# First chunk of an mLSTM cell with a feed-forward block: another order of weight parts, values and quarters, and sums of three with fewer copies

## The chip, the cores and the metric

The kernel runs on one core of a Trainium2 chip. The metric is device time in microseconds (us) of that core, the median of several executions. A profile of one execution gives the start, length and releaser of each instruction on each engine: TensorE (PE; its weight loads are PEld), VectorE (DVE), ScalarE (ACT), GpSimd (POOL) and SyncE (SP), which issues the transfers.

## The reference, cut to what matters

An mLSTM cell runs over 768 steps for 4 batches of 8 heads with 40 values each; its output, seen as 3072 rows of 320, goes through two matrices of weights with a quick GELU between them. All inputs are float32.

```python
for t in range(S):                                  # S = 768; B = 4, H = 8, D = 40
    kt, vt, qt = (k[:, :, t], v[:, :, t], q[:, :, t])
    m_new = np.maximum(f_gate[:, :, t] + m, i_gate[:, :, t])
    f_stab = np.exp(f_gate[:, :, t] + m - m_new)
    i_stab = np.exp(i_gate[:, :, t] - m_new)
    m = m_new
    C = f_stab[:, :, None, None] * C + i_stab[:, :, None, None] * np.einsum('bhd,bhe->bhde', vt, kt)
    n = f_stab[:, :, None] * n + i_stab[:, :, None] * kt
    h_tilde = np.einsum('bhde,bhe->bhd', C, qt)
    nq = np.einsum('bhd,bhd->bh', n, qt)[:, :, None]
    y[:, :, t] = h_tilde / np.maximum(np.abs(nq), 1.0) / (1.0 + np.exp(-o_gate[:, :, t]))
x = y.transpose(0, 2, 1, 3).reshape(B * S, H * D)   # 3072 x 320
h = x @ w_in                                        # w_in 320 x 2048
out = (h / (1.0 + np.exp(-1.702 * h))) @ w_out      # w_out 2048 x 320
```

## The kernel before, in words

The 768 steps are cut into 6 chunks (`w`) of 128. Within a chunk the recurrence is written as attention: for each batch `b`, `weights(w, b)` gives the decay of each pair of steps, `scores(w, b)` the products of keys and queries on TensorE, which VectorE multiplies into the decay (L353), and `values(w, b)` the products of that with v (L363), followed on VectorE by the denominator and the output gate (L390 to L396) and on POOL by a copy of the last 64 columns of the row `y` (L398). `seam(w, b)` transposes `y` on TensorE (L405) and ScalarE copies it into the columns of batch `b` in `xT` (L406). The feed-forward block follows: `up` and then `down`. From chunk 1 on, both products are run by a scheme with seven products instead of eight, and the attention of the next chunk is run between the blocks of `down`.

The order of the instructions on each engine is the order in which the program names them; every engine has its own queue and works it off in that order, and waits are put where one instruction needs another's data or buffer. All that the change touches lies in the first chunk, whose calls stand one after another at L665 to L736.

The first chunk has its own ways. Keys and queries of batch `b` are transposed on TensorE into PSUM and copied by ScalarE (`transposes(0, b)`, L308 and L311). The decay is formed on TensorE from two rows of numbers, minus the gate sum `a3` and the running maximum `m3`, each held as a sum of three bfloat16 on 3 times 32 partitions, and ScalarE takes the exponential (L325 to L331). `gates(0)` makes these sums of three: POOL those of `a3` (L252 to L256), VectorE those of `m3` (L262 to L267). Each part is made in `part`, copied to its 32 partitions, and subtracted from what is left.

The matrices of weights come as float32 and are converted on the chip, in 20 pieces of 128 x 512. `convert(n, "A")` is ScalarE's part of a piece (L228, the high half, and L229, the low half), `convert(n, "V")` is VectorE's (L232 to L237), which needs both; `convert(n)` names both parts. SP issues the loads of all pieces in one queue together with those of k, q, v and the gates, and pieces 10 and later are loaded into the room of earlier ones once these are converted.

For the first two column blocks of `up` the kernel doesn't wait for all four batches: `full_rows(j, c, t)` multiplies the rows of two batches (half `t`) for one block `j` and one of two parts `c` of the inner dimension, two matmuls of 256 columns in a call (L713), which the profile lists as four records (a float32 product is listed twice). The four calls of half 0 are called its quarters here. Part `c` = 0 needs weight piece 0, part `c` = 1 piece 1. The rest of the inner dimension, 64 of 320, is added by L736 from piece 2. `keep_busy(n)` runs `n` matmuls of 128 x 512 on zeros whose result isn't used.

PSUM tiles of the attention come from one pool, `ps_a`, with four buffers, so that a product on TensorE can also wait for the engine that reads an older one.

Of the kernel before, what the change touches and what calls it, by code (L numbers as in the profile page):

```python
# [12 lines left out]
OP = mybir.AluOpType  # L13
# [21 lines left out]
def kernel(  # L35
# [14 lines left out]
    BH = B * H  # L50
# [134 lines left out]
    def keep_busy(n, pool=ps_a, tag="a"):  # L185
        p_idle = pool.tile([128, W], FP, tag=tag, name="p_idle")
        for _ in range(n):
            T.matmul(p_idle, idle, idle.unsqueeze(1).to_broadcast([128, 4, 128]), start=True, stop=True)
# [34 lines left out]
    def convert(n, engines="AV"):  # L223

        lo, hi, dst = bits[n][:, :, 0], bits[n][:, :, 1], pieces[n][0]
        dst_u = dst.bitcast(U32)
        if "A" in engines:
            A.activation(out=dst, in_=hi.bitcast(FP), func=AF.Abs)  # L228
            A.activation(out=lo, in_=lo, func=AF.Copy, scale=2.0 ** -29)  # L229
        if "V" not in engines:  # L230
            return
        V.tensor_scalar(out=dst, in0=dst, scalar1=HI_MIN, scalar2=HI_MAX, op0=OP.max, op1=OP.min)  # L232
        V.tensor_scalar(out=dst_u, in0=dst_u, scalar1=3, scalar2=0x3FFFFFFF, op0=OP.logical_shift_left,
                        op1=OP.bitwise_and)
        V.scalar_tensor_tensor(out=dst_u, in0=hi, scalar=0xC0000000, in1=dst_u, op0=OP.bitwise_and,
                               op1=OP.bitwise_or)
        V.tensor_tensor(out=dst_u, in0=dst_u, in1=lo, op=OP.add)  # L237


    def gates(w):  # L240
        m = m_at[w]
        f_run = gate.tile([BH, L], FP, bufs=1, name="f_run")
        m_run = gate.tile([BH, L], FP, bufs=1, name="m_run")
        st = stacked[w] = gate.tile([3 * BH, L], FP, name="st")
        V.tensor_tensor_scan(out=f_run, data0=ones, data1=f_sb[w], initial=0.0, op0=OP.mult, op1=OP.add)
        a = st[0:BH, :]
        V.tensor_tensor(out=a, in0=i_sb[w], in1=f_run, op=OP.subtract)
        if w == 0:
            room = work.tile([L, H, D1], FP, tag="u", name="room").rearrange("p h d -> p (h d)")
            neg, part = room[0:BH, 0:L], room.bitcast(BF)[0:BH, 2 * L:3 * L]  # L250
            V.tensor_tensor(out=neg, in0=f_run, in1=i_sb[w], op=OP.subtract)
            for j in range(3):  # L252
                G.tensor_copy(out=part, in_=neg)
                G.tensor_copy(out=a3[j * BH:(j + 1) * BH, :], in_=part)
                if j < 2:
                    G.tensor_tensor(out=neg, in0=neg, in1=part, op=OP.subtract)  # L256
        V.tensor_tensor_scan(out=m_run, data0=ones, data1=a, initial=m, op0=OP.mult, op1=OP.max)
        if w == 0:

            room = work.tile([L, H, D1], FP, tag="u", name="room").rearrange("p h d -> p (h d)")  # L260
            left, part = room[0:BH, 0:L], room.bitcast(BF)[0:BH, 2 * L:3 * L]
            for j in range(3):  # L262
                rest = left if j else m_run
                V.tensor_copy(out=part, in_=rest)
                V.tensor_copy(out=m3[j * BH:(j + 1) * BH, :], in_=part)
                if j < 2:
                    V.tensor_tensor(out=left, in0=rest, in1=part, op=OP.subtract)  # L267
        else:
            m_row[w] = rows.tile([BH, L], FP, name="m_row")
            nc.sync.dma_start(out=m_row[w], in_=m_run)  # L270
        end = m_run[:, L - 1:L]
        if w + 1 < NW:
            m_at[w + 1] = gate.tile([BH, 1], FP, name="m_end")
            V.tensor_tensor(out=m_at[w + 1], in0=f_run[:, L - 1:L], in1=end, op=OP.add)

        V.tensor_scalar(out=st[BH:2 * BH, :], in0=m_run, scalar1=m, scalar2=None, op0=OP.subtract)
        V.tensor_scalar(out=st[2 * BH:3 * BH, :], in0=a, scalar1=end, scalar2=-1.0, op0=OP.subtract, op1=OP.mult)
        if 0 < w < NW - 1:
            dec[w] = dec_in[:, w % 2, :]
            both = gate.tile([BH, 1], FP, name="both")  # L280
            V.tensor_tensor(out=both, in0=m, in1=end, op=OP.subtract)
            V.tensor_scalar(out=dec[w][0:BH, :], in0=pair, scalar1=both, scalar2=None, op0=OP.mult)
# [15 lines left out]
    def transposes(w, b, which=slice(0, 2)):  # L298
        for bl, st, dst, name in ((k_bl, k_st, kT, "kT"), (q_bl, q_st, qT, "qT"))[which]:
            dst[w, b] = work.tile([128, NP, L], FP, tag=name, bufs=4, name=name)  # L300
            if w:
                V.transpose(out=dst[w, b].rearrange("p j t -> p (j t)"),
                            in_=bl[:, b * NP:(b + 1) * NP].rearrange("p j g c -> p (j g c)"))
                continue
            pt = ps_a.tile([128, NP, L], FP, tag="a", name="p_t")
            for p in range(NP):
                h = b * H + 2 * p
                T.transpose(pt[:, p, :], st[:, h:h + 2, :].rearrange("p a b -> p (a b)"), ident)  # L308
            if b == 0:
                keep_busy(1)  # L310
            A.copy(out=dst[w, b], in_=pt)  # L311
# [8 lines left out]
    def weights(w, b):  # L320
        if w == 0:
            x = wt[w, b] = work.tile([L, NP, 2, L], FP, tag="wt", bufs=4, name="wt")
            for i in range(2):
                pw = ps_a.tile([L, NP, L], FP, tag="a", name="p_w")
                T.matmul(pw, ident_bf, not_yet.unsqueeze(1).to_broadcast([L, NP, L]), start=True, stop=False)  # L325
                for p in range(NP):
                    h = b * H + 2 * p + i
                    one = pick[:, h:h + 1].to_broadcast([3 * BH, L])
                    T.matmul(pw[:, p, :], one, m3, start=False, stop=False)
                    T.matmul(pw[:, p, :], a3, one, start=False, stop=(p == NP - 1))  # L330
                A.activation(out=x[:, :, i, :], in_=pw, func=AF.Exp)  # L331
            return
        x = wt[w, b].rearrange("s p i t -> s (p i) t")
        for h in range(H):
            A.activation(out=x[:, h, :], in_=x[:, h, :], func=AF.Exp, scale=-1.0,  # L335
                         bias=cols[w][:, b * H + h:b * H + h + 1])
        G.affine_select(out=x, in_=x, compare_op=OP.is_ge, fill=0.0, base=0, pattern=[[0, H], [1, L]],  # L337
                        channel_multiplier=-1)
        if w > 1 and b == 0:
            gates_out(w)  # L340
# [4 lines left out]
    def scores(w, b):  # L345
        pool, tag = (ps_x, "x") if w > 1 and b % 2 == 0 else (ps_a, "a")
        pw = [pool.tile([L, NP, L], FP, tag=tag, name="p_s") for _ in range(2)]
        for p in range(NP):
            for i in range(2):
                r = slice(i * 64, i * 64 + D)  # L350
                T.matmul(pw[i][:, p, :], kT[w, b][r, p, :], qT[w, b][r, p, :], start=True, stop=True)
        for i in range(2):
            V.tensor_tensor(out=wt[w, b][:, :, i, :], in0=pw[i], in1=wt[w, b][:, :, i, :], op=OP.mult)  # L353
# [46 lines left out]
    def seam(w, b):  # L400
        if b == 0:
            xT[w] = work.tile([128, 3, B, L], FP, tag="xT", bufs=1, name="xT")
        px = ps_a.tile([128, 3, L], FP, tag="a", name="p_x")
        for c in range(3):
            T.transpose(px[:, c, :], ys[w, b][:, c * 128:(c + 1) * 128], ident)  # L405
        A.copy(out=xT[w][:, :, b, :], in_=px)  # L406
# [277 lines left out]
    gate_out(0)  # L684
    gate_out(1)
    values(0, 0)
    convert(0, "A")
    values(0, 1)
    transposes(0, 2)
    weights(0, 2)  # L690
    seam(0, 0)
    seam(0, 1)
    convert(0, "V")
    scores(0, 2)
    transposes(0, 3)
    convert(1, "A")
    weights(0, 3)
    convert(1, "V")
    scores(0, 3)
# [10 lines left out]
    def full_rows(j, c, t):  # L710
        ts = slice(t * (W // 2), (t + 1) * (W // 2))
        for i in range(2):
            T.matmul(first[j][i][:, ts], w_half[i][c][:, 0, j * 128:(j + 1) * 128], x_first[:, c, ts],  # L713
                     start=(c == 0 and t == 0), stop=True, skip_group_check=True)

    full_rows(0, 0, 0)
    full_rows(1, 0, 0)
    values(0, 2, states=True)
    values(0, 3, states=True)
    convert(2, "A")  # L720
    full_rows(0, 1, 0)
    full_rows(1, 1, 0)
    seam(0, 2)
    keep_busy(2)
    seam(0, 3)
    keep_busy(2)
    convert(2, "V")
    convert(3)
    convert(4)
# [135 lines left out]
```

## Time and profile before

| what | value |
|---|---|
| median of 4 runs | 486.85 us (486.58 to 486.93) |
| the profiled execution | 486.71 us, its span 485.0 us |
| first chunk's quarters for half 0 | 24.17 to 26.09 us and 28.02 to 30.01 us |
| values of batches 2 and 3 | 26.02 to 28.09 us |
| seams 2 and 3, each with two idle matmuls | 29.85 to 31.52 us |
| quarters for half 1 begin | 31.66 us |
| ScalarE busy from 14 to 32 us | 10.80 of 18 us |
| VectorE busy from 14 to 32 us | 14.58 of 18 us |

The profile gives times from the start of the span. A line of the order of time reads: start, length of all that it merges, engine, line, operation, output and inputs, number of instructions, and in brackets the idle time of the engine before it with what ended that time. Lengths of matmuls include the time in which they drain, so neighbours overlap. A line of waits reads: who waited for whom, total us, how often, and the longest.

### The profile page before, as it was taken

Reading aid. Unit: us, or ns where it says so; the run is one execution under the profiler, and the core shown is the slowest. Engines: PE = TensorE matmul, PEld = TensorE weight load, DVE = VectorE, ACT = ScalarE, POOL = GpSimd, SP = SyncE. Lnnn points to the kernel's source line nnn. Section 1 sums busy time; section 2 is a strip of 40 time slices with the busy share of each in tenths; the row PEclk is TensorE's granted clock in tenths of the full one; section 3 lists DMA queues with packets and bytes.
Section 4 is the critical chain, followed back from the end, with each engine's and each line's share of the span. In section 5 each row is a group of like instructions: output and inputs, shape, how many; then the busy total and the mean of one; then the engine's idle time right before and its main releaser. Section 6 shows DMA issues by size and latency. Waiting matters only on the chain. (4 is left out here: it accounts for less than half of the span.)

```text
span 485.0 us, 10445 instructions
## 1 busy us (share of the span) xinstructions
PE 479.3 (99%) x4076; PEld 397.5 (82%) x4076; DVE 343.1 (71%) x855; ACT 220.6 (45%) x575; POOL 61.7 (13%) x103
## 2 busy tenths in 40 slices
PE   8999999999999999999999999999999999999997
PEld 5874457777779999788999877999877999977997
DVE  8788879887978965667766677696576786254831
ACT  6757767303649302467600465900374920255300
POOL 4030002420000430000331000332000120000000
PEclk9999999999999999999999999999999999999999
DMA  9999779934996100996100896200492000000000
GB/s 127 216 301 298 166 140 229 113 48 72 162 206 77 9 30 28 184 182 79 7 29 15 120 252 67 28 28 3 83 261 23 1 15 16 28 1 0 1 27 28
DMA packets 175953, 44.87 MB, mean 93 GB/s; under 512 B 164352, under 2 KB 169504, under 8 KB 175904
## 3 DMA queue, kind: packets, MB, share of 16 engines
q1 hardware_dynamic: 175328, 43.55, 49.0%
q8 instruction: 32, 0.52, 0.5%
q10 hardware_dynamic: 576, 0.66, 0.4%
q14 instruction: 17, 0.14, 0.1%
HBM read 40.17 MB, written 4.01 MB: 91 GB/s over the span
## 5 line engine op out<-in xcount | busy, mean ns | idle before, releaser
L616 PE MATMUL p_out<-w_out_sb,g 128*128 128x160 f32 x480 | 69.8, 301 | 0.0
L406 ACT COPY xT<-p_x 128x384 f32<-128x384 f32 x24 | 10.8, 481 | 125.9 <-PE p_x L405 112.8
L616 PEld LDWEIGHTS p_out<-w_out_sb,g 128*128 128x128 f32 x480 | 66.3, 190 | 0.9
L527 DVE TENSOR_TENSOR g<-p_u,g 128x256 f32<-128x256 f32 x80 | 33.7, 425 | 44.6 <-PE p_u L519 35.0
L524 ACT COPY g<-p_u 128x256 f32<-128x256 f32 x120 | 43.1, 377 | 43.5 <-PE p_u L519 39.3
L531 ACT ACTIVATE g<-g 128x256 f32<-128x256 f32 x120 | 42.3, 425 | 39.3 <-DVE g L527 39.3
L337 POOL TENSOR_SCALAR_AFFINE_SELECT wt<-wt 128x1024 f32<-128x1024 f32 x20 | 22.8, 1139 | 235.0 <-ACT wt L335 235.0
L621 DVE TENSOR_TENSOR o_sb<-o_sb,p_out 128x160 f32<-128x160 f32 x70 | 21.4, 317 | 42.2 <-PE p_out L616 41.8
L335 ACT ACTIVATE wt<-wt,cols 128x128 f32<-128x128 f32 x160 | 47.8, 393 | 0.0
L519 PE MATMUL p_u<-xT,w_in_sb 128*128 128x256 f32 x160 | 38.9, 382 | 0.0
L519 PE MATMUL p_u<-xs,big 128*128 128x256 f32 x160 | 37.9, 379 | 0.0
L547 PE MATMUL p_u<-xT,w_in_x 64*128 64x512 f32 x80 | 37.0, 602 | 0.0
L547 PE MATMUL p_v<-xT,w_in_x 64*128 64x512 f32 x80 | 37.0, 602 | 0.0
L353 DVE TENSOR_TENSOR wt<-p_s,wt 128x512 f32<-128x512 f32 x48 | 30.4, 682 | 9.0 <-POOL wt L337 6.7
L567 PE MATMUL p_out<-w_out_sb,g 128*128 128x320 f32 x128 | 36.3, 436 | 0.0
L616 PE MATMUL p_out<-t,big 128*128 128x160 f32 x240 | 35.5, 301 | 0.0
L519 PEld LDWEIGHTS p_u<-xT,w_in_sb 128*128 128x128 f32 x160 | 29.6, 190 | 5.4 <-DVE o_sb L621 1.5
L519 PEld LDWEIGHTS p_u<-xs,big 128*128 128x128 f32 x160 | 30.0, 190 | 4.6 <-ACT g L524 0.2
L616 PEld LDWEIGHTS p_out<-t,big 128*128 128x128 f32 x240 | 33.3, 190 | 0.2
L567 PEld LDWEIGHTS p_out<-w_out_sb,g 128*128 128x128 f32 x128 | 23.8, 190 | 9.8 <-issue 0.5
L527 DVE TENSOR_TENSOR g<-p_v,g 128x256 f32<-128x256 f32 x80 | 29.8, 415 | 0.0
L547 PEld LDWEIGHTS p_v<-xT,w_in_x 64*128 64x128 f32 x80 | 14.2, 186 | 16.0 <-issue 16.0
(168 smaller groups left out, 861.5 us busy)
## 6 DMA issues: line engine op xcount, KB each, us to landing
wt<-m_row SPq DMA_DIRECT2D x20, 512.0 KB, 6.8
v_st<-in_v_dram SPq DMA_DIRECT2D x5, 640.0 KB, 8.9
eo<-in_o_gate_dram SPq DMA_DIRECT2D x5, 640.0 KB, 5.6
k_st<-in_k_dram SPq DMA_DIRECT2D x5, 640.0 KB, 11.1
out_dram<-o_sb SPq DMA_DIRECT2D x20, 160.0 KB, 1.8
big<-in_moe_w_in_dram SPq DMA_DIRECT2D x5, 512.0 KB, 6.7
k_bl<-in_k_dram SPq DMA_DIRECT2D x40, 64.0 KB, 2.8
q_bl<-in_q_dram SPq DMA_DIRECT2D x40, 64.0 KB, 2.6
```

The lines of the kernel that those rows point to most:

```text
L335: A.activation(out=x[:, h, :], in_=x[:, h, :], func=AF.Exp, scale=-1.0, bias=cols[w][:, b * H + h:b * H + h + 1])
L337: G.affine_select(out=x, in_=x, compare_op=OP.is_ge, fill=0.0, base=0, pattern=[[0, H], [1, L]], channel_multiplier=-1)
L353: V.tensor_tensor(out=wt[w, b][:, :, i, :], in0=pw[i], in1=wt[w, b][:, :, i, :], op=OP.mult)
L406: A.copy(out=xT[w][:, :, b, :], in_=px)
L519: T.matmul(p[k][:, ts[t]], a[:, k // 2, k % 2 * 128:(k % 2 + 1) * 128], b, start=first, stop=True, skip_group_check=True)
L524: A.copy(out=g[k][i][:, ts[t]], in_=chain[k][:, ts[0]])
L527: V.tensor_tensor(out=g[k][i][:, ts[t]], in0=p[k][:, ts[pt]], in1=g[k][i][:, ts[t]], op=OP.add)
L531: A.activation(out=dst, in_=dst if src is None else src, func=AF.Gelu_apprx_sigmoid)
L547: T.matmul(p[k], w_in_x[r, k, :], x[r, 2, :], start=False, stop=True, skip_group_check=True)
L567: T.matmul(po, gs[w, f // 2][:, f % 2, b * L:(b + 1) * L], w_out_sb[:, f, :], start=(f == 0), stop=(f == NF - 1))
L616: T.matmul(po, a(f), b[:, f, :], start=(f == 0), stop=(f == NH - 1))
L621: V.tensor_tensor(out=dst, in0=x, in1=po, op=OP.add)
```

## The change

Four things are changed, all in the first chunk.

- The sums of three are made by a new helper, `in_three`. The first part is converted straight into its partitions and subtracted from there, the second is made in `part` and copied, the third is converted straight into its partitions: six operations instead of eight. POOL does it for `a3`, VectorE for `m3`.
- ScalarE's part of weight piece 0 stands behind `transposes(0, 2)` instead of between the values of batches 0 and 1; that of piece 1 stands ahead of `transposes(0, 3)` instead of behind it.
- The values of batches 2 and 3 stand ahead of the first two quarters instead of behind them.
- The last two quarters of half 0 stand one behind each of the seams 2 and 3, where four idle matmuls stood, which are gone.

```diff
+    def in_three(E, three, x, left, part):
+
+        E.tensor_copy(out=three[0:BH, :], in_=x)
+        E.tensor_tensor(out=left, in0=x, in1=three[0:BH, :], op=OP.subtract)
+        E.tensor_copy(out=part, in_=left)
+        E.tensor_copy(out=three[BH:2 * BH, :], in_=part)
+        E.tensor_tensor(out=left, in0=left, in1=part, op=OP.subtract)
+        E.tensor_copy(out=three[2 * BH:3 * BH, :], in_=left)
+
     def gates(w):
...
             V.tensor_tensor(out=neg, in0=f_run, in1=i_sb[w], op=OP.subtract)
-            for j in range(3):
-                G.tensor_copy(out=part, in_=neg)
-                G.tensor_copy(out=a3[j * BH:(j + 1) * BH, :], in_=part)
-                if j < 2:
-                    G.tensor_tensor(out=neg, in0=neg, in1=part, op=OP.subtract)
+            in_three(G, a3, neg, neg, part)
...
             left, part = room[0:BH, 0:L], room.bitcast(BF)[0:BH, 2 * L:3 * L]
-            for j in range(3):
-                rest = left if j else m_run
-                V.tensor_copy(out=part, in_=rest)
-                V.tensor_copy(out=m3[j * BH:(j + 1) * BH, :], in_=part)
-                if j < 2:
-                    V.tensor_tensor(out=left, in0=rest, in1=part, op=OP.subtract)
+            in_three(V, m3, m_run, left, part)
...
     values(0, 0)
-    convert(0, "A")
     values(0, 1)
     transposes(0, 2)
+    convert(0, "A")
     weights(0, 2)
     seam(0, 0)
     seam(0, 1)
     convert(0, "V")
     scores(0, 2)
+    convert(1, "A")
     transposes(0, 3)
-    convert(1, "A")
     weights(0, 3)
     convert(1, "V")
     scores(0, 3)
...
+    values(0, 2, states=True)
+    values(0, 3, states=True)
     full_rows(0, 0, 0)
     full_rows(1, 0, 0)
-    values(0, 2, states=True)
-    values(0, 3, states=True)
     convert(2, "A")
+    seam(0, 2)
     full_rows(0, 1, 0)
+    seam(0, 3)
     full_rows(1, 1, 0)
-    seam(0, 2)
-    keep_busy(2)
-    seam(0, 3)
-    keep_busy(2)
     convert(2, "V")
     convert(3)
     convert(4)
```

## The prediction

> **What bounds the kernel now.** I read the page's first two parts, then the list of what TensorE waited for over the whole span, then the order of time of the first chunk.
>
> ```profile
> PE 479.3 (99%) x4076; PEld 397.5 (82%) x4076; DVE 343.1 (71%) x855; ACT 220.6 (45%) x575; POOL 61.7 (13%) x103
> ...
> PE   8999999999999999999999999999999999999997
> ...
> PEclk9999999999999999999999999999999999999999
> ```
>
> TensorE is busy 99% of the span. Its list of waits has only five entries, and four of them lie in the first 18 us:
>
> ```profile
> PE p_idle L188 <- DVE idle L182: 1.1, 1, 1.1
> PE p_out L616 <- DVE o_sb L621: 0.4, 1, 0.4
> PE p_w L325 <- ACT kT L311: 0.3, 1, 0.3
> PE p_t L308 <- DMA k_st<-in_k_dram: 0.3, 1, 0.3
> PE p_w L330 <- POOL a L254: 0.2, 1, 0.2
> ```
>
> So the change is worth what it moves one event: the start of the matmuls on the second half of the rows (L713, x16) at 31.66 us. Behind it TensorE runs without a recorded wait to 411.6 us, so an earlier or later start there shifts the end by as much. The orders of time around it, engine by engine (start, length, engine, line):
>
> ```profile
> 24.17 1.92 PE L713 MATMUL p_h<-xT,w_in_sb 128*128 128x256 f32 x8
> 26.02 2.07 PE L363 MATMUL p_o<-v_st,wt 128*64 128x41 f32 x64
> 28.02 1.99 PE L713 MATMUL p_h<-xT,w_in_sb 128*128 128x256 f32 x8
> 29.85 0.49 PE L405 MATMUL p_x<-ident,y 128*128 128x128 f32 x3
> 30.18 0.59 PE L188 MATMUL p_idle<-idle 128*128 128x512 bf16 x2
> 30.61 0.49 PE L405 MATMUL p_x<-ident,y 128*128 128x128 f32 x3
> 30.93 0.59 PE L188 MATMUL p_idle<-idle 128*128 128x512 bf16 x2
> 31.66 3.72 PE L713 MATMUL p_h<-xT,w_in_sb 128*128 128x256 f32 x16
> ```
>
> ```profile
> 16.23 0.68 ACT L228 ACTIVATE w_in_sb<-big 128x512 f32<-128x512 f32 x1 [2.48 <-DMA big<-in_moe_w_in_dram]
> ...
> 18.31 1.13 ACT L331 ACTIVATE wt<-p_w 128x512 f32<-128x512 f32 x2
> ...
> 21.28 0.59 ACT L311 COPY kT<-p_t 128x512 f32<-128x512 f32 x1 [1.08 <-PE p_t L308]
> ```
>
> ```profile
> 22.94 0.43 DVE L232 TENSOR_SCALAR w_in_sb<-w_in_sb 128x512 f32<-128x512 f32 x1 [0.99 <-ACT w_in_sb L228]
> ...
> 25.30 1.28 DVE L353 TENSOR_TENSOR wt<-p_s,wt 128x512 f32<-128x512 f32 x2
> 27.20 0.17 DVE L390 TENSOR_SCALAR den<-p_o 128x8 f32<-128x8 f32 x1 [0.61 <-PE p_o L363]
> ```
>
> The reader is to see that in this stage TensorE is filled (quarters of the up product, values, transposes, four idle matmuls), while ScalarE stands still 1.08 us before 21.28 and VectorE 0.99 us before 22.94, waiting for ScalarE's part of weight piece 1.
>
> **The change part by part.** Sums are made against the profiled execution, 486.71 us (its span is 485.0), 0.14 under the median of 486.85.
>
> *Sums of three with fewer copies.* Each of POOL and VectorE loses two copies of eight operations. On POOL the steps that go are 4.87 to 5.13 and 7.07 to 7.42, so a3 is ready near 7.1 instead of 7.71. On VectorE the two that go are rows of 0.20 and 0.41 us, of which the next start gains some 0.4. TensorE's 0.2 wait for a3 goes and weights(0, 0) end up to 0.4 earlier. Then it is lost: gates(1) on VectorE start at 8.84 on the landing of the second forget gates (issued at 4.33, 4.5 us to landing), VectorE is unbroken from there to 12.45 through the multiplication by scores(0, 0), and scores(0, 1) need the buffer which that frees. Bounds: zero, and a gain of 0.4 if the landing were not the limit. I take 0, as the trace names the landing. The converting copy into partitions 64 to 95 has no row of its own; the nearest (0.21 to 0.33 on VectorE, 0.28 to 0.41 on POOL) lie under the same cover.
>
> *convert(0, "A") behind transposes(0, 2).* Its two instructions take 1.15 us from start to next start (16.23 to 17.38). The transposes of keys end at 16.54, so the copy of kT starts at 16.6, qT at 17.06 (spacing 0.46), the conversion runs 17.53 to 18.66, the two exponentials 18.66 to 19.79. Before, they ended at 19.44: ScalarE has lost the 0.35 between the landing of the piece and the end of the transposes. TensorE's 0.35 wait for kT at 17.99 goes, but its next step, scores(0, 2) at 19.40, needs the buffer of the second exponential: its second row group can start at 19.85 instead of 19.50, and it ends near 20.98 instead of 20.65. A loss of 0.33 here, between 0 (if the wait removed counts) and 0.35. The copies of seams 0 and 1 come 0.35 later too. VectorE's convert(0, "V") starts near 18.25 instead of 17.58 and ends at 20.7, still before scores(0, 2) are ready.
>
> *convert(1, "A") ahead of transposes(0, 3).* The piece was issued at 13.12 and took 7.1 to land: 20.2. It runs in ScalarE's idle time, 20.5 to 21.65. Queued behind it is the copy of kT for batch 3, whose transposes now end near 21.6: no cost, 0.2 at most. VectorE loses its 0.99 wait: multiplication (0, 2) 21.0 to 22.28, conversion of piece 1 from 22.2 instead of 22.94, multiplication (0, 3) 2.36 later at 24.56 instead of 25.30, done at 25.85 instead of 26.58.
>
> *Last values ahead of the quarters.* With scores(0, 3) 0.33 later, columns run at 24.36 and values(0, 2) at 24.5 to 25.5; their v landed at 21.1 (issue 16.04, 5.1). values(0, 3) need the multiplication that ends at 25.85: TensorE stands 0.4, a new wait with all four quarters queued behind it, then goes on to 26.95. VectorE's two tails (1.47 each by the rows from 27.20 to 28.67) run 25.8 to 28.7, POOL's last copy of y to 29.0 instead of 30.65. The output gate of batch 3 lands at 25.68 and its tanh ends at 26.15, before VectorE needs it near 27.7.
>
> *Quarters between the seams, no idle matmuls.* From 26.95: two quarters 1.92, seam 2 0.33, a quarter 0.96, seam 3 0.33, a quarter 0.96, together 4.50: 31.45. Both y are ready 1.2 us or so before their seams, and seam 3's copy ends near 31.0, so the second half finds its rows waiting. What goes is the four idle matmuls, 0.215 each by the spacing of their row, 0.86, and what hid under them: the copy of xT, now covered by the quarters. Without that cover a copy costs 0.72 (seam start 30.61 to 31.66, less the 0.33 of its own issue).
>
> *convert(2, "A") on ScalarE* stays ahead of both seams' copies, released by its landing at 27.85 and done at 29.09, when seam 2 is just due (29.2): cost 0 to 0.1. convert(2, "V") starts near 28.7 instead of 30.13 and the pieces that up needs follow earlier. No transfer is moved past another in SP's queue; its first refill of a piece's room was at 30.02, after both conversions in either order.
>
> Sum: 31.45 against 31.66, that is 0.2 earlier: 0.86 of idle matmuls gone, against 0.33 at scores(0, 2), and the rest of the difference at values(0, 3). Profiled 486.5, median 486.65. If the 0.33 doesn't appear, 31.15 and 0.5 earlier.
>
> One rule speaks against the change. The granted clock is 1.00 in every stretch of this profile, with idle matmuls and without them, also where TensorE stood 0.35 at 17.99. The Trainium skill, "TensorE: Matmul & The Clock Gate", section "Why this matters for your kernels", says that a pause of over some 3 us brings half clock, and in "Part 4: PE-mode transpose" that transposes don't count as busy; if the seams counted as such a pause, one window of 3.4 us (its Part 1) at half clock would cost 1.7 us and give about 488.4, an estimate from that page that no run here shows. The sum goes by the rows: the longest new wait is 0.4, and matmuls lie between the transposes.
>
> **The rivals.** *The new wait doesn't appear.* If VectorE's chain is 0.4 to 0.7 earlier than I have it, because scores(0, 2) aren't held by the second exponential, TensorE runs from 17.64 with only its own work: 31.66 less 0.86, less 0.35, is 30.45, 1.2 earlier: 485.65. For it speaks that TensorE has little other idle time there; against it, that ScalarE does the same work 0.35 later, and VectorE alone needs 21.95 + 2.36 + 1.28 = 25.6 for the last multiplication even without that.
>
> *Quarters wait for the seam's copy (slower).* full_rows(0, 1, 0) comes behind seam(0, 2), which writes other columns of the same tile xT. If the wait is for the whole tile, TensorE stands 0.72 after each seam: 28.87 + 1.05 + 0.96 + 1.05 + 0.96 is 32.89, 1.23 later than before: 488.1. It decides as soon as both seams wait. Against it: the matmuls of 24.17 read one part of w_in_sb while VectorE writes another (24.70), and POOL's memset of k_st's padding ran at 1.31, far before the load of the same tile landed.
>
> *No gain at all:* the idle matmuls only filled a wait for y, and the tails are as late as before. That gives 486.85; but y would have to slip 1.2 us.
>
> **How the numbers follow.** Forecast 486.65 with its own range of 486.2 to 486.95: 0.53. The wait that doesn't appear, 485.65: 0.22. No gain, up to 0.5 slower: 0.10. Seam copies, 488.1: 0.12. A lower clock, which no row of this profile prices: 0.03. The range 485.4 to 487.6 leaves out the last two. 0.2% is 0.97 us, about what a measurement of this kernel tells from no change; the first and third cases lie within, the second mostly beyond: faster 0.23, same 0.62, slower 0.15.
>
> **What would show it.** Right: no idle time before VectorE's second conversion, exponentials of (0, 2) ending near 19.8, a wait of TensorE of about 0.4 in values(0, 3) on the multiplication, L713's x16 at 31.1 to 31.5. Wrong: a wait of TensorE on the copy of xT after 28.9, a granted clock under 1.00, or values that start later than 24.6.

## The result, and the profile after

The changed kernel takes 485.88 us (median of 42 runs, 485.65 to 486.96) against 486.92 us before (60 runs, 486.47 to 487.57): a ratio of 0.998, with a 95% interval of 0.9976 to 0.9984. It is 1.04 us faster, at the edge of the 0.2% that was named as the least that can be told from no change. Forecast were 486.65 us and 0.2 us: the result lies within the whole range of 485.4 to 487.6, but below the forecast's own range of 486.2 to 486.95.

The profiled execution took 485.91 us with a span of 484.2 us; that of before took 486.71 with 485.0. So 0.80 us of the 1.04 can be followed from line to line. TensorE's list of waits over the whole span, after (who waited for whom, total us, times, longest):

```profile
PE p_idle L188 <- DVE idle L182: 1.1, 1, 1.1
PE p_t L307 <- DMA k_st<-in_k_dram: 0.5, 1, 0.5
PE p_out L615 <- DVE o_sb L620: 0.4, 1, 0.4
PE p_s L350 <- ACT wt L330: 0.4, 1, 0.4
```

The waits for kT and for a3 are gone, and a wait of 0.4 us of the scores of batch 2 for the exponential is new. The order of time on TensorE, after (start, length, engine, line):

```profile
19.31 1.64 PE L350 MATMUL p_s<-qT,kT 40*128 40x128 f32 x16 [0.36 <-ACT wt L330]
...
24.34 0.30 PE L285 MATMUL p_cols<-ident,st 96*128 96x96 f32 x1
24.58 2.30 PE L362 MATMUL p_o<-v_st,wt 128*64 128x41 f32 x64
26.80 1.99 PE L712 MATMUL p_h<-xT,w_in_sb 128*128 128x256 f32 x8
28.64 0.49 PE L404 MATMUL p_x<-ident,y 128*128 128x128 f32 x3
28.96 1.03 PE L712 MATMUL p_h<-xT,w_in_sb 128*128 128x256 f32 x4
29.83 0.49 PE L404 MATMUL p_x<-ident,y 128*128 128x128 f32 x3
30.16 4.48 PE L712 MATMUL p_h<-xT,w_in_sb 128*128 128x256 f32 x20
34.57 1.99 PE L733 MATMUL p_h<-xT,w_in_x 64*128 64x512 f32 x8
36.49 3.70 PE L463 MATMUL p_h<-xT,w_in_sb 128*128 128x512 f32 x8
```

Before, three of these places were at:

```profile
24.03 0.30 PE L286 MATMUL p_cols<-ident,st 96*128 96x96 f32 x1
...
35.32 1.99 PE L736 MATMUL p_h<-xT,w_in_x 64*128 64x512 f32 x8
37.23 3.70 PE L464 MATMUL p_h<-xT,w_in_sb 128*128 128x512 f32 x8
```

The matmuls into `p_cols`, called columns here, are the last work on TensorE ahead of the stretch whose order is changed. They run 0.31 us later than before, and the values that now follow them start at 24.58. From there to the matmuls of the rest (the last 64 of the inner dimension) at 34.57 nothing but TensorE's own work is in the way, except for a pause of about 0.2 within the values of batch 3: four of their 32 records run up to 25.60, the next one starts at 25.86, when the multiplication has ended (25.80). The last quarter and the second half stand in one row (x20 from 30.16): by its spacing of 0.216 a record, the second half starts four records in, at 31.02, where it had been 31.66. The matmuls of the rest (L733) start at 34.57, where they had been at 35.32, and the next pair of blocks at 36.49 instead of 37.23. The gain of 0.75 is complete here, and the span shows 0.8 at the end.

VectorE and ScalarE, after:

```profile
20.84 1.29 DVE L352 TENSOR_TENSOR wt<-p_s,wt 128x512 f32<-128x512 f32 x2 [0.18 <-PE p_s L350]
22.05 0.42 DVE L232 TENSOR_SCALAR w_in_sb<-w_in_sb 128x512 f32<-128x512 f32 x1
...
24.51 1.29 DVE L352 TENSOR_TENSOR wt<-p_s,wt 128x512 f32<-128x512 f32 x2
```

```profile
16.55 0.59 ACT L310 COPY kT<-p_t 128x512 f32<-128x512 f32 x1 [3.23 <-PE p_t L307]
...
17.51 0.68 ACT L228 ACTIVATE w_in_sb<-big 128x512 f32<-128x512 f32 x1
...
18.68 1.05 ACT L330 ACTIVATE wt<-p_w 128x512 f32<-128x512 f32 x2
...
20.71 0.68 ACT L228 ACTIVATE w_in_sb<-big 128x512 f32<-128x512 f32 x1 [0.23 <-DMA big<-in_moe_w_in_dram]
```

VectorE's 0.99 us of waiting ahead of its second conversion is gone, and the multiplication of batch 3 starts at 24.51 instead of 25.30. ScalarE's first weight part starts at 17.51 instead of 16.23, and its second exponential ends at 19.73 instead of 19.44.

### The profile page after: what moved, and what is told of

It is laid out like the page before. It is cut to its first block, busy times and chain, and to the rows that moved or that the text cites. A ratio compares the mean times of both kernels' runs of the same rounds, so it can differ in the third digit from the quotient of the medians.

```text
span 484.2 us, 10432 instructions
## 1 busy us (share of the span) xinstructions
PE 478.6 (99%) x4072; PEld 397.3 (82%) x4072; DVE 343.1 (71%) x853; ACT 220.8 (46%) x575; POOL 60.6 (13%) x101
```

## The experiments

The question was which of the four parts carries the gain. The theory of the interplay says: TensorE's queue bounds the stretch, and the gain needs both that work goes from it (the idle matmuls) and that the values needn't wait. Against it stands that one part alone carries it. Times are medians; each group was timed beside the kernel before on the same chip.

### Each part alone

Idle matmuls alone:

```diff
     seam(0, 2)
-    keep_busy(2)
     seam(0, 3)
-    keep_busy(2)
```

> The kernel before, only without the four idle matmuls at seams 2 and 3. Theory of the interplay (no part alone gains; the parts together shorten TensorE's queue): the last row y is complete only at 30.65 us, so seam 3 and its copy end where they did, and the second half starts at 31.6 to 31.7: no change (0, at most 0.1 faster). Rival (the idle matmuls alone were the cost): 0.4 to 0.9 us faster.

Measured: 486.90 against 486.88 us, ratio 0.9999 (0.9990 to 1.0008). The order of time on TensorE in this run:

```profile
30.04 1.18 PE L405 MATMUL p_x<-ident,y 128*128 128x128 f32 x6
31.79 3.72 PE L713 MATMUL p_h<-xT,w_in_sb 128*128 128x256 f32 x16 [0.57 <-ACT xT L406]
```

The idle matmuls turned into an idle engine: 0.57 us of waiting for the copy of xT. They had covered a wait, so that taking them away gives nothing by itself.

Sums of three alone (the helper and its two calls as in the change):

> The kernel before, only with the sums of three made in six operations. Theory: the decay of batch 0 is ready 0.4 us earlier, and VectorE still starts the second gates when they land (8.84) and the first multiplication at 11.2: no change (0 to 0.1). Rival (the front of the chunk is carried through): 0.3 to 0.5 us faster.

Measured: 486.87 against 486.88 us, 1.0002 (0.9994 to 1.0011). No change, as expected. The start of the second gates on VectorE, in the profile of the kernel before and in that of the changed one, shows where the earlier sums end:

```profile
8.84 0.41 DVE L245 TENSOR_TENSOR_SCAN f_run<-one,fi 32x128 f32<-32x128 f32 x1 [0.18 <-DMA fi<-in_f_gate_dram]
```

```profile
8.85 0.41 DVE L254 TENSOR_TENSOR_SCAN f_run<-one,fi 32x128 f32<-32x128 f32 x1 [0.69 <-DMA fi<-in_f_gate_dram]
```

ScalarE's two weight parts alone (their two moves as in the change):

> The kernel before, only with ScalarE's parts of weight pieces 0 and 1 moved. Theory of the interplay: VectorE's multiplication of batch 3 ends 0.75 us earlier, but TensorE reaches the values only behind the first two quarters, now 0.3 later, and the second half starts 0.3 later: 0.1 to 0.4 us slower. Rival (the weight parts carry the gain): 0.3 to 0.8 faster.

Measured: 486.95 against 486.88 us, 1.0003 (0.9995 to 1.0012). No gain; the loss of 0.07 us lies within the interval, under the 0.1 to 0.4 expected. The profile shows why nothing is won. VectorE is early, but waits:

```profile
27.96 0.17 DVE L390 TENSOR_SCALAR den<-p_o 128x8 f32<-128x8 f32 x1 [1.71 <-PE p_o L363]
```

The 0.99 us that VectorE had waited ahead of its conversion is gone, but its wait ahead of the denominators has grown from 0.61 to 1.71 us, because TensorE still does two quarters ahead of the values. (This execution took 487.40 us, 0.45 above the median: its piece 1 landed late, as told below.)

The order on TensorE alone (values, quarters, seams and no idle matmuls as in the change):

> The kernel before, only with the last values ahead of the quarters, the quarters between the seams, and no idle matmuls. Theory of the interplay: values of batch 3 wait for the multiplication that ends at 26.58, about 0.8 to 1.3 us of TensorE, and the second half starts at 31.6 to 31.8: no change (0.1 faster to 0.2 slower). Rival (the order alone carries the gain, as it takes 0.86 us of work from TensorE): 0.6 to 0.9 us faster.

Measured: 487.00 against 486.88 us, 1.0013 (1.0002 to 1.0024): no gain. That the ratio lies above 1 comes mostly from three of the twelve executions, 488.34, 488.72 and 489.81 us, whose mean granted clock (1 is full speed) was 0.996, 0.996 and 0.992; the other nine took 486.85 to 487.28. No profile shows where these three lost the clock. TensorE's waits have the line that tells why nothing is gained:

```profile
PE p_o L363 <- DVE wt L353: 0.6, 1, 0.6
```

The values of batch 3 wait for the multiplication, and all four quarters behind them. The 0.6 is only the idle time ahead of batch 3. From the start of the values to that of the first quarter TensorE took 3.09 us (24.82 to 27.91), where the same values took 2.00 without a wait (26.02 to 28.02 before): 1.1 us of waiting, within the expected 0.8 to 1.3. So none of these four edits gains alone: the theory of the interplay stands, and each rival that named one of them falls. Not run was the move of piece 1 alone, without that of piece 0.

### Which parts are needed together

The changed kernel with the sums of three as before:

> The changed kernel with the sums of three made as before, in eight operations. Theory (what the sums gain ends at the landing of the second gates): as fast as the changed kernel, 0.8 to 1.1 us faster than before. Rival (the sums carry part of the gain once the rest is changed): 0.3 to 0.5 slower than the changed kernel.

Measured: 485.90 against 486.94 us, 0.9981 (0.9972 to 0.9990). The sums do nothing in company either.

The changed kernel with ScalarE's part of piece 0 back at its old place:

```diff
     values(0, 0)
+    convert(0, "A")
     values(0, 1)
     transposes(0, 2)
-    convert(0, "A")
```

> The changed kernel, only with ScalarE's part of piece 0 back between the values of batches 0 and 1. First theory (as predicted: the move itself costs 0.33 at the scores of batch 2): 0.2 to 0.4 us faster than the changed kernel, so 1.2 to 1.4 faster than before. Second theory (the move is an insurance against the landing of piece 0, which came between 16.2 and 17.3 us in the profiles so far): the copy of kT follows the landing by 1.15, the second exponential ends at landing plus 3.2, which equals the changed kernel's 19.7 for a landing of 16.5; 0.3 faster to 0.7 slower than the changed kernel from execution to execution, median within 0.2 of it, and a wider spread.

Measured: 485.93 against 486.96 us, 0.9981 (0.9972 to 0.9990), as fast as the changed kernel (485.88). The first theory, that the move itself costs 0.33 us, falls. The piece landed at 16.37 here, TensorE waited 0.5 us for kT, the second exponential ended at 19.60 and columns ran at 24.18, against 19.73 and 24.34 in the changed kernel: what the move costs at the exponential it saves at kT, but for 0.16 us at this landing. The second theory's median came true, its wider spread didn't show (485.38 to 486.67, against 485.65 to 486.96).

The changed kernel with the part of piece 1 back behind the transposes of batch 3:

```diff
-    convert(1, "A")
     transposes(0, 3)
+    convert(1, "A")
```

> The changed kernel with ScalarE's part of piece 1 back behind the transposes of batch 3. Theory (the earlier part of piece 1 is what lets VectorE end the multiplication of batch 3 early enough for values that stand ahead of the quarters): that multiplication ends near 26.9 instead of 25.8, TensorE waits 1.0 to 1.4 for it, the second half starts at 31.9 to 32.2: 0.9 to 1.2 us slower than the changed kernel, and so 0.2 faster to 0.2 slower than before. Rival (the order on TensorE alone carries the gain once the copies of batch 2 are early): as fast as the changed kernel.

Measured: 486.97 against 486.94 us, 1.0002 (0.9994 to 1.0011): the whole gain is gone. VectorE, and what TensorE then waits for:

```profile
23.07 0.43 DVE L232 TENSOR_SCALAR w_in_sb<-w_in_sb 128x512 f32<-128x512 f32 x1 [1.10 <-ACT w_in_sb L228]
25.43 1.28 DVE L352 TENSOR_TENSOR wt<-p_s,wt 128x512 f32<-128x512 f32 x2
```

```profile
24.62 1.13 PE L362 MATMUL p_o<-v_st,wt 128*64 128x41 f32 x32 [0.16 <-ACT wt L330]
26.38 1.41 PE L362 MATMUL p_o<-v_st,wt 128*64 128x41 f32 x32 [0.62 <-DVE wt L352]
27.72 2.00 PE L712 MATMUL p_h<-xT,w_in_sb 128*128 128x256 f32 x8
```

VectorE's wait for the part is back, and the multiplication ends at 26.71. The values took 3.10 us from their start to that of the first quarter, against 2.00 without a wait: 1.1 us of waiting, as expected (1.0 to 1.4). The 0.62 in the line is a part of it; after four records the row of batch 3 waits again, from 26.46 to 26.77, for the second half of the multiplication. The loss in time is as expected too.

The kernel before with only the part of piece 1 ahead of the transposes of batch 3 and the new order on TensorE:

> The kernel before with two of the four parts alone: ScalarE's part of piece 1 ahead of the transposes of batch 3, and the new order of values, quarters and seams without idle matmuls. Theory (these two are the whole of the gain): as fast as the changed kernel within 0.2, 0.8 to 1.1 us faster than before. Rival (all four are needed): 0.3 or more slower than the changed kernel.

Measured: 485.87 against 486.94 us, 0.9979 (0.9970 to 0.9988). These two are the whole gain; the sums of three and the move of piece 0 added nothing that can be told from zero.

### Is TensorE the bound?

The changed kernel with four idle matmuls, two behind each of the quarters between the seams:

```diff
     full_rows(0, 1, 0)
+    keep_busy(2)
     seam(0, 3)
     full_rows(1, 1, 0)
+    keep_busy(2)
```

> The changed kernel with the four idle matmuls put back, two behind each quarter between the seams. Theory (TensorE's own work bounds the stretch from the last values to the second half): four times 0.216, 0.86 us slower than the changed kernel, and so 0 to 0.2 us faster than before. Rival (TensorE has slack there, and the gain came from elsewhere): as fast as the changed kernel, 0.8 to 1.0 faster than before.

Measured: 486.77 against 486.96 us, 0.9997 (0.9989 to 1.0006), 0.89 us above the changed kernel. Work of 0.86 us on TensorE costs its full time there: this stretch has no slack left.

### The landing of piece 0

In the profiles with the old place of its part, piece 0 landed between 16.23 and 17.25 us, and the execution with the latest landing, that of the sums alone, took 487.65 us where its median is 486.87. ScalarE's start and TensorE's wait in it:

```profile
17.25 0.67 ACT L228 ACTIVATE w_in_sb<-big 128x512 f32<-128x512 f32 x1 [3.95 <-DMA big<-in_moe_w_in_dram]
```

```profile
PE p_w L325 <- ACT kT L311: 1.4, 1, 1.4
```

In all six profiles with the old place columns run 7.80 us behind the start of that part, within 0.01: at 24.03 for 16.23 (the kernel before), at 24.18, 24.23, 24.30 and 24.36 for 16.37, 16.43, 16.50 and 16.56, and at 25.05 for 17.25. So a later landing goes through in full there.

To see what a later landing costs in either order, the load of piece 0 was put behind those of the last keys and queries, in the kernel before and in the changed one:

```diff
-... ("kq", 2), (fetch, 0), ("kq", 3), (fetch, 1), ...
+... ("kq", 2), ("kq", 3), (fetch, 0), (fetch, 1), ...
```

> The kernel before, with the load of weight piece 0 issued behind those of the last keys and queries instead of ahead of them, some 1.3 us later. Theory (the copies of batch 2 stand behind ScalarE's wait for this piece, so every delay of the landing goes through to the second half and the end): the piece lands at 17.5 to 18.7, 1.0 to 2.2 us slower than before. Rival (the landing has slack): 0 to 0.3 slower.

> The changed kernel with the same later load of piece 0. Theory (the copies of batch 2 stand ahead of the wait now; the piece is only needed by 17.5): a landing at 17.5 to 18.7 costs 0 to 1.0 us against the changed kernel, at least 0.9 less than the same delay costs the kernel before; 1.0 faster to 0.2 slower than before. Rival (both orders wait for the landing alike): 1.0 to 2.2 us slower than the changed kernel, 0 to 1.2 slower than before.

Measured: 492.02 us in the order before (1.0103, 1.0090 to 1.0116) and 489.75 us in the changed one (1.0068, 1.0044 to 1.0092), both against 486.96. In the order before the delay costs 5.1 us, in the changed one 3.9 (against 485.88), so the changed order bears the delay with 1.2 us less, which the theory had put at 0.9 or more. But both losses are far above what was expected. The landing itself was later (ScalarE's part starts at 19.35 in the one, 18.93 in the other), and then the clock fell. Of the changed order with the late load, the stretches of one us from 18 to 23 (busy times of the five engines, then the granted clock, DMA share, GB/s):

```profile
core 0: us, PE busy (x) PEld busy (x) DVE busy (x) ACT busy (x) POOL busy (x), PEclk, DMA share, GB/s
18.00:19.00 1.00, 0.77 (x9) 0.54 (x6) 0.00 (x0) 0.07 (x1) 0.00 (x0) 1.00 1.08 360
19.00:20.00 1.00, 0.00 (x0) 0.00 (x0) 0.37 (x1) 1.00 (x2) 0.00 (x0) 1.00 1.29 246
20.00:21.00 1.00, 0.31 (x2) 0.29 (x2) 0.93 (x3) 1.00 (x3) 0.00 (x0) 1.00 0.66 100
21.00:22.00 1.00, 1.00 (x10) 0.82 (x10) 0.86 (x2) 1.00 (x4) 0.00 (x0) 0.55 1.03 175
22.00:23.00 1.00, 1.00 (x10) 0.95 (x8) 0.13 (x2) 0.99 (x2) 0.00 (x0) 0.50 0.85 175
```

TensorE stood from 18.77 to 20.69; the mean of 0.55 from 21 to 22 puts the drop to half clock near 21.1, and it stays there to 27.9 (0.50 in each us to 27, 0.54 from 27 to 28). So a part of these two losses is the clock's, and they don't measure the landing alone.

The mean clocks of the single executions allow a comparison at an equal loss of clock. At a mean of 0.996 the order before took 491.21 and 491.28 us, 4.3 above its own median, and the changed one 488.89 to 489.14, 3.2 above its own. At 0.993 they took 492.75 and 492.78 (5.8 above) and 490.37 and 490.83 (4.7 above). (A sixth execution of the changed order had 0.986 and 493.39 us.) So the clock doesn't explain the difference, which is 1.1 us at an equal mean. That the piece landed 0.42 us later in the profile of the order before may be a part of it.

### A try for a faster version

The changed kernel with the second gates behind weight piece 4, their row written out ahead of the loads of the next keys, and piece 1 loaded ahead of the last keys and queries:

```diff
-    gates(1)
     scores(0, 0)
...
     convert(4)
+    gates(1)
...
-... (fetch, 0), ("kq", 3), (fetch, 1), ...
+... (fetch, 0), (fetch, 1), ("kq", 3), ...
```

> A try for a faster version: the changed kernel with the second gates made behind weight piece 4 (their row is written out ahead of the loads of the next keys), and the load of piece 1 ahead of those of the last keys and queries. Theory (VectorE then starts the first multiplication at 10.6 instead of 11.2, and the chain of multiplications with it): the second half starts 0.3 to 0.6 earlier, 1.2 to 1.6 us faster than before. Rival (the last keys and queries land too late for their transposes at 20.9, and TensorE waits): 0 to 1.5 us slower than the changed kernel.

Measured: 485.83 against 486.94 us, 0.9981 (0.9972 to 0.9989): the same as the changed kernel. VectorE and TensorE in the first steps, then where it was lost:

```profile
10.44 1.29 DVE L357 TENSOR_TENSOR wt<-p_s,wt 128x512 f32<-128x512 f32 x2 [2.29 <-PE p_s L355]
```

```profile
17.45 0.68 ACT L228 ACTIVATE w_in_sb<-big 128x512 f32<-128x512 f32 x1 [0.42 <-DMA big<-in_moe_w_in_dram]
```

```profile
19.22 1.64 PE L355 MATMUL p_s<-qT,kT 40*128 40x128 f32 x16 [0.88 <-ACT wt L335]
```

The first multiplication is 0.75 us earlier (10.44 instead of 11.19), but ScalarE then waits for piece 0, and the scores of batch 2 wait 0.88 for the exponential behind it. The gain ended at the landing of a piece, 7 us further on.

## Why the prediction was right or wrong

**The bound.** Right. A start 0.75 us earlier at 36.49 arrived as 0.8 us at the end of the span, and 0.86 us of idle matmuls put back cost 0.89.

**Sums of three: 0.** Right, in both settings. VectorE was idle 0.69 us before the second gates instead of 0.18, so the earlier m3 ended in that wait.

**Piece 0 behind the transposes.** The steps were right almost to the row: kT at 16.55 (16.6 forecast), the part at 17.51 (17.53), the second exponential's end at 19.73 (19.79), columns at 24.34 (24.36). What it is worth was not. The 0.33 was charged to the move as if the old place had no such cost in other executions, while the profiled landing of 16.23 was the earliest of the six that were seen at that place (up to 17.25). With the part at its old place and the rest changed the time is the same. By the 7.80 us from landing to columns, the changed kernel's 24.34 is what the old place gives for a landing at 16.54, and three of the six were at 16.43 to 16.56.

**Piece 1 ahead of the transposes.** Right: the wait of 0.99 is gone and the multiplication ends at 25.80 (25.85 forecast). It is the necessary part. The wait behind its landing was given as "no cost, 0.2 at most". It depends on the landing, which the part now meets ahead of kT: in the four profiles with both parts moved and SP's loads unchanged (the changed kernel, the sums as before, the two parts alone, the idle matmuls added), ScalarE starts it at 20.71, 21.05, 21.18 and 21.66, and columns run at 24.34, 24.67, 24.79 and 25.26, always 3.6 us later. The last three executions took 0.34, 0.45 and 1.12 us more than their kernels' medians.

**Values and quarters.** Here the sum went wrong, in the sizes; the waits and the path were those of the forecast. A quarter was taken as 0.96 us, half of a row's length of 1.92, which includes the last matmul's drain; its four records follow each other at 0.216, which is 0.864 (only the first record behind the values took 0.32). From the end of the values, two quarters and seam 2, a quarter, seam 3 and a quarter were to take 4.50 and took 4.22 (26.80 to 31.02). The values with their wait were to take 2.45 and took 2.22: the new wait cost 0.2 and not 0.4. The multiplication ended where it was forecast, but the sum let all values of batch 3 wait for its end, while the first four of their 32 records need only its first half and ran ahead of the pause. That is 0.51 us, less 0.08 because the values started later; the second half started at 31.02, where 31.45 was forecast and 31.1 to 31.5 named as the sign of being right. Another 0.11 came where the second half no longer begins with a wait for the copy of xT: from its start to the matmuls of the rest it took 3.66 us before and 3.55 after. The runs show that this is the wait's and not the idle matmuls': 3.66 with the wait alone (idle matmuls taken out, 31.79 to 35.45), 3.55 with idle matmuls and no wait (the four put back, 32.80 to 36.35). Forecast 0.2 earlier and 0.43 and 0.11 make the 0.75.

**The rest, 0.24 of 1.04.** The profiled execution of before lay 0.21 us under the median of its 60 runs, that of the changed kernel 0.03 above its own. The likely cause is the landing of piece 0, which was early in the former: columns follow it at 7.80 us, and the middle of the six landings, 16.47, is 0.24 later than its 16.23. That the 60 runs lie the same way is argued, not shown.

**The rivals.** "The new wait doesn't appear" came to 485.65 us, nearer to the result than the forecast, but by a mechanism that didn't happen, so that its number came close by luck: both waits were there, that for the exponential at 19.31 and that of the values for the multiplication. "Quarters wait for the seam's copy" is excluded by the profile: transposes and quarters follow each other from 28.64 to 34.57 at their own spacing. "No gain at all" described each part alone, and not the four together. The granted clock of the changed kernel was 1.00 throughout its profile, as forecast, and 0.999 or more in all 42 executions.

## What to carry to other kernels

Edits of which none moves the time alone can still be worth doing: the work taken from the bounding engine pays only if the wait that it was covering is removed with it, so try such edits in pairs before dropping them. Then take them out again one by one: here two of the four could have been left out. For the sum of an engine's queue use the spacing from start to start, not the length of a merged row, which holds the drain of its last instruction; here that was 0.28 us of 4.50. The idle time that a profile gives ahead of a merged row isn't the whole wait either (0.62 of 1.1 us with piece 1 put back); compare the time from start to start with that of the same work where nothing waits. A copy that is queued behind a wait for a transfer inherits the scatter of the landing, so look at that landing in more than one execution before pricing the move.

## What the runs showed of the hardware

In the changed order with the late load the clock was lost for longer than the pause that lost it. TensorE did transposes of y from 17.95 to 18.77, stood 1.92 us, began the scores at 20.69 with two records and went on at 21.18, when their second exponential had ended; from 21.1 it had half clock for 6.8 us. In the order before with the late load it waited 3.5 us (the wait for kT in its list) up to 21.1, and had half clock from about 21.2 to 24.6 (means of 0.60 and 0.69 in the stretches at the two ends, 0.50 between), 3.4 us. A wait of 0.4 us in the changed kernel and one of 1.4 with the sums alone left the clock at 1.00.

The length isn't the order's: of the executions above, the profile with 3.4 us of half clock has a mean clock of 0.996 and that with 6.8 us one of 0.993, and both means came up in both orders. The second 3.4 us cost 1.5 us in the order before (491.25 to 492.77) and 1.6 in the changed one (489.04 to 490.60), an estimate from the means of the executions at each clock. The clock also fell in one of the eleven executions with the part of piece 1 put back (0.996, 488.48 us), besides the three with the order alone.

The Trainium skill, "TensorE: Matmul & The Clock Gate", section "Why this matters for your kernels", names pauses of over some 3 us; here the longest single wait was 1.92 us, and the clock fell all the same. Its "Part 4: PE-mode transpose", that transposes don't count as busy, would make one pause from 17.95 to 20.69, 2.7 us, nearer to that figure but still under it. No run here separates the transposes from the waits on either side of 20.69.
